# A fourth PV ahead of the second half, and first scores within the projections: a fused attention and SwiGLU layer on one core

## The chip, the cores and the metric

The kernel runs on one core of a Trainium2 chip. The metric is device time in microseconds of one execution, the median of several runs. The engines are named as in the profile: PE (matmuls), PEld (PE's weight loads), DVE (vector), ACT (scalar, activations), POOL (GpSimd) and SP (which issues most DMAs; "SPq" and "ACTq" are the issuing of DMAs).

## The reference

```python
# x [1, 2048, 576], wqkv [576, 1728], wo [576, 576], w1 and w3 [576, 4608], w2 [4608, 576], all bf16
xn = layernorm(x)
q, k, v = heads(xn @ wqkv)                  # 32 heads of 18
s  = q @ k.T * 18 ** -0.5                   # causal, window of 256 keys
A  = concat(softmax(s) @ v) @ wo
B  = (silu(xn @ w1) * (xn @ w3)) @ w2
out = x + A + B
```

## The kernel before

The 2048 tokens are done in four chunks of 512. A chunk has these stages on PE, in this order:

1. The projections (`proj_part`, L437): four pairs of q and k tiles, four of v, and one last k tile, in the order of `PROJ` (L462): q0, q1, v0, q2, v1, q3, v2, 8, v3. Every projection is cut in two parts: the second part of one is issued behind the first part of the next. They use pairs of 64-row tiles of the array.
2. Gate/up (`unit_pairs`, L668): 36 units, each nine pairs of 64-row matmuls of 512 columns. ACT takes a tanh of a unit's gate (`unit_tanh`), DVE makes hT of it with two operations (`unit_h`).
3. The second half (`p2_list`, `p2_item`): full-array matmuls hT by w2 (L719) and oT by wo (L725), 288 columns each, for two halves of the output columns and four blocks of 128 tokens. The wo matmuls come at the end of each half. Four PSUM banks, `ACC`, hold the four sums.

The attention of the chunk is woven into this stream. The heads go in 8 groups of 4. A group has 5 score steps (4 in chunk 0); a step is a few matmuls of 64-row tiles (`scores`, L561) into two fixed banks `SC` = (6, 7), an exp on ACT (`exps`, L570), and masks on POOL (`masks`, L597). Two groups share one PV (`pv`, L618: 96 small matmuls of tiles of 64 rows by 20 columns, 72 in chunk 0). So there are four PVs in a chunk, and behind each a chain on DVE and POOL (`pv_out`, `o_scale`, `o_turn`) and DMAs (`o_pack`) that bring the result into oT, which the wo matmuls read.

A planner written into the kernel sets the order at build time, with a `clock` that counts pairs of 512 columns. It puts a score step into the stream when the clock has passed `nxt`; `nxt` begins at `start`, and the steps are spread so that they are done by `last`:

```python
            start = 20 if c == 0 else 46
            last = total - 12
```

The check stands once behind each entry of `PROJ` (L903 to L917) and ahead of every pair of gate/up. The first three PVs are placed between gate/up units; the fourth stands within the second half, behind its 20th item, in banks taken from a ring of the last two units' banks.

The other six banks form three pairs, `JOBS`, that `job()` hands out in turn to projections, units and PVs.

Before a group can be scored, its queries and keys are moved by DMA: DVE and ACT copy a q pair from PSUM to `stage`, then `repack_span` moves them: `span_main` (L502) and `span_last` (L533). For group 0 these are two DMAs on ACT for the queries, with the semaphore q_0, and four on SP for the keys, with the semaphore k_0; they are issued when q0's second part has been recorded, and the first score of a later chunk waits for all of them. Instructions of one engine run in the order in which they were recorded.

Of the kernel before, what the change touches and what calls it, by code (L numbers as in the profile page):

```python
# [44 lines left out]
class _Prog:  # L45
# [13 lines left out]
    def add(self, eng, fn, r=(), w=(), j=(), dma=None, after=()):  # L59
        deps = []  # L60
        for k in r:
            deps += self.bufs[k].writers
        for k in w:
            g = self.bufs.get(k)
            if g is not None:
                deps += g.ahead(eng)
        for k in j:
            g = self.bufs[k].before
            if g is not None:
                deps += g.ahead(eng)  # L70
        op = _Op(eng, fn, deps + list(after), dma)
        op.after = tuple(after)
        self.n[eng] += 1
        op.pos = self.n[eng]
        if dma is not None:
            self.dma_count[dma] = self.dma_count.get(dma, 0) + 16
            op.cnt = self.dma_count[dma]
        for k in r:
            self.bufs[k].readers.append(op)
        for k in w:  # L80
            self.bufs[k] = _Gen([op], self.bufs.get(k))
        for k in j:
            self.bufs[k].writers.append(op)
        for k in w:
            if self.bufs[k].before is not None:
                self.bufs[k].before.before = None
        self.ops.append(op)
        return op
# [76 lines left out]
def bass_parallel_sum__sliding_block__glu_gated_swiglu__prompt_kernel(  # L165
# [21 lines left out]
    NF = F // 128  # L187
# [10 lines left out]
    with ExitStack() as es:  # L198
# [32 lines left out]
        def pt_slot(sl):  # L231
            kind, n = sl
            if kind == "pt":
                return pt[:, n, :, :]
            if kind == "sh":
                two = stage[:, 2 * n:2 * n + 2, :]
            else:
                two = hT[:, NF - 8 + 2 * n:NF - 6 + 2 * n, :]
            return two.rearrange("p t c -> p (t c)").rearrange("p (q r) -> p q r", r=2)

        def pt_keys(sl):
            kind, n = sl
            if kind == "pt":
                return [("pt", n)]
            if kind == "sh":
                return [("sh", 2 * n), ("sh", 2 * n + 1)]
            return [("h", NF - 8 + 2 * n), ("h", NF - 7 + 2 * n)]
# [16 lines left out]
        PS = es.enter_context(nc.psum_tensor("ps", [128, 8, 512], dt.float32))  # L264
        JOBS, SC = ((0, 1), (2, 3), (4, 5)), (6, 7)
        ACC = [4, 5, 6, 7]
        ring_of = [0, 1, 2, 3]
        ring_ctr = 2
        job_ctr = 2

        def ring():
            nonlocal ring_ctr
            i = ring_of[ring_ctr % 4]
            ring_ctr += 1
            return i

        def job():
            nonlocal job_ctr
            i = job_ctr % 3
            job_ctr += 1  # L280
            return JOBS[i]
# [13 lines left out]
        def load_x(t, eng="sp"):  # L295
            nonlocal xp_ctr
            s = xp_ctr % NXP
            xp_ctr += 1
            add(eng, lambda e: e.dma_start(xp[s][:], x2[t * 128:(t + 1) * 128, :]), w=[("xp", s)], dma=f"xp{s}")
            return s  # L300
# [239 lines left out]
        def keep_keys(g):  # L540
            add("pool", lambda e: e.tensor_copy(
                kb4[:, g, :, :].bitcast(dt.float32), kv[:, g, 2 * NB - NV:NB, :].bitcast(dt.float32)),
                r=[("k", g)], w=[("kp", g)])
# [3 lines left out]
        def steps_of(c):  # L547

            if c == 0:
                return [[(0, 0, 5), (5, 5, 3)], [(1, 1, 5), (6, 6, 2), (7, 7, 1)],  # L550
                        [(2, 2, 5), (4, 4, 2)], [(3, 3, 5), (4, 6, 2)]]
            return [[(0, 0, 5), (-2, 0, 3)], [(1, 1, 5), (5, 5, 3)], [(2, 2, 5), (-3, 0, 2), (-4, 0, 1)],
                    [(3, 3, 5), (6, 6, 2), (7, 7, 1)], [(-1, 0, 4), (4, 4, 4)]]
# [46 lines left out]
        def pv(c, j, banks):  # L600

            seen = set()
            n_all = sum(len(st) for st in steps_of(c))
            n = 0
            for s, st in enumerate(steps_of(c)):
                col = 0
                for kb, q0, nb in st:
                    n += 1
                    pos = (c * NB + kb) % NV
                    for gi in range(2):  # L610
                        g = 2 * j + gi
                        sl = pt_of[(c, g, s)]
                        for pr in range(2):
                            for p in range(2):
                                first = (p, gi, pr) not in seen
                                seen.add((p, gi, pr))
                                q = 2 * gi + pr
                                add("pe", lambda e, p=p, q=q, pr=pr, sl=sl, g=g, pos=pos, q0=q0, nb=nb, col=col, first=first, n=n: e.matmul(  # L618
                                    PS[32 * q:32 * q + VW, banks[p], q0 * KB:(q0 + nb) * KB],
                                    va[64 * p:64 * p + 64, pos, g, pr, :],  # L620
                                    pt_slot(sl)[64 * p:64 * p + 64, col * KB:(col + nb) * KB, pr],
                                    start=first, stop=(n == n_all), tile_position=(64 * p, 32 * q), skip_group_check=True),
                                    r=pt_keys(sl) + [("va", pos)], **{"j" if any(k[0] == p for k in seen - {(p, gi, pr)}) or not first else "w": [("ps", banks[p])]})
                    col += nb

        def pv_out(b, i):
            add("dve", lambda e: e.transpose(uqs[i], PS[:, b, :]), r=[("ps", b)], w=uq_keys[i])
# [63 lines left out]
        def p2_list(c):  # L691

            seq = []
            for half in range(2):
                base = c * 2 * NFC + half * NFC
                for fc in range(NFC):
                    sl = (base + fc) % NW2
                    edge = fc == NFC - 1 or (half == 1 and fc == 0)
                    pairs = [(fl, tt) for fl in range(4) for tt in range(TB)]
                    if edge:  # L700
                        pairs = [(fl, tt) for tt in range(TB) for fl in range(4)]
                    for n, (fl, tt) in enumerate(pairs):
                        seq.append(("w2", half, fc, fl, tt, sl, n == len(pairs) - 1))
                        if fc == NFC - 1 and fl == 3:
                            seq += [("wo", half, fc, kd, tt, sl, False) for kd in range(5)]
                            seq.append(("out", half, fc, 0, tt, sl, False))
            return seq
# [142 lines left out]
        for c in range(NC):  # L850
# [6 lines left out]
            total = 9 * NF + len(att) + 3 * PV_COST  # L857
            if c:
                total += 9 * sum(COST[kind] for kind, _ in PROJ)
            start = 20 if c == 0 else 46  # L860
            last = total - 12
            nxt = soon = start
            clock = 0.0
            done = 0
            pv_ready = {}
# [5 lines left out]
            jobs = {}  # L871
# [47 lines left out]
            for u in range(NF):  # L919
# [18 lines left out]
                if next_pv in pv_ready and clock >= pv_ready[next_pv] and next_pv < 3:  # L938
                    j = next_pv
                    next_pv += 1  # L940
                    banks = job()
# [34 lines left out]
                if u == 29:  # L976
                    xs = [load_x(c * TB + tt) for tt in range(TB)]
            assert done == len(att) and next_pv == 3, (done, next_pv)
            ring_of[:] = [*jobs[NF - 2], *jobs[NF - 1]]
            ring_ctr = 0  # L980
            ACC[:] = [*job(), *SC]
            assert len({*ring_of, *ACC}) == 8
            if c + 1 < NC:
                for g in range(G):
                    keep_keys(g)
            banks = ()
            for n, item in enumerate(p2_list(c)):
                p2_item(c, item, xs)
                if n == 3:
                    for u in sorted(side):  # L990
                        for what in side.pop(u):
                            what()
                elif n == 19:
                    banks = (ring(), ring())
                    pv(c, 3, banks)
                    pv_out(banks[0], 0)
                    pv_out(banks[1], 1)
                    o_scale(0)
                    o_turn(6, 0)
                    o_turn(6, 1)  # L1000
                    o_scale(1)
                    o_turn(7, 0)
                    o_turn(7, 1)
                    o_pack(3, "act")
                elif n == 40 and c + 1 < NC:
                    xn_send((c + 1) * TB + 3)
                elif n == 300 and c + 1 < NC:
                    xn_swap(c + 1, ("sp", "sp"))
                elif n in (100, 120) and c + 2 < NC:
                    t = (c + 2) * TB + (n == 120)  # L1010
                    xslot[t] = load_x(t)
# [31 lines left out]
```

## Time and profile before

| | us |
|---|---|
| median of 3 runs | 564.06 |
| lowest, highest | 564.05, 564.6 |
| the profiled execution | 562.96 |
| its span, first to last instruction | 561.3 |

| engine | busy us | share of the span |
|---|---|---|
| PE | 555.2 | 99% |
| PEld | 330.0 | 59% |
| DVE | 315.9 | 56% |
| ACT | 253.3 | 45% |
| POOL | 163.9 | 29% |

PE's granted clock is full throughout. By line, PE is busy 332.3 us with gate/up (L668), 147.1 with the w2 matmuls (L719), 51.2 with scores (L561), 38.3 with the projections (L437) and 24.8 with wo (L725). Overlapping matmuls count once in a group, and their ends are modelled, so a place on PE is best read by the starts of its matmuls. The stages of chunk 1 in the trace: projections from 144.69 us, the first score at 155.29, gate/up's first pair at 158.30, the second half from 240.96, the fourth PV at 243.51, the end at 282.6.

### The profile page before, as it was taken

Reading aid. Unit: us, or ns where it says so; the run is one execution under the profiler, and the core shown is the slowest. Engines: PE = TensorE matmul, PEld = TensorE weight load, DVE = VectorE, ACT = ScalarE, POOL = GpSimd, SP = SyncE. Lnnn points to the kernel's source line nnn. Section 1 sums busy time; section 2 is a strip of 40 time slices with the busy share of each in tenths; the row PEclk is TensorE's granted clock in tenths of the full one; section 3 lists DMA queues with packets and bytes.
Section 4 is the critical chain, followed back from the end, with each engine's and each line's share of the span. In section 5 each row is a group of like instructions: output and inputs, shape, how many; then the busy total and the mean of one; then the engine's idle time right before and its main releaser. Section 6 shows DMA issues by size and latency. Waiting matters only on the chain.

```text
span 561.3 us, 15707 instructions
## 1 busy us (share of the span) xinstructions
PE 555.2 (99%) x6765; PEld 330.0 (59%) x6765; DVE 315.9 (56%) x586; ACT 253.3 (45%) x349; POOL 163.9 (29%) x384
## 2 busy tenths in 40 slices
PE   7999999999999999999999999999999999999998
PEld 3544544677655455477755545547776454555776
DVE  7666788710366778851046668884114567767211
ACT  3476666100286766600038677650004676666000
POOL 6433344400033445430003444533000333433000
PEclk9999999999999999999999999999999999999999
DMA  9986969965566477596546655969563674460552
GB/s 246 220 171 159 205 171 202 226 177 158 130 142 139 113 162 157 130 214 179 158 106 139 161 123 126 162 162 205 156 172 69 137 172 123 123 162 12 138 148 64
DMA packets 126565, 85.83 MB, mean 153 GB/s; under 512 B 33976, under 2 KB 124272, under 8 KB 126496
## 3 DMA queue, kind: packets, MB, share of 16 engines
q1 hardware_dynamic: 124469, 82.39, 63.0%
q10 hardware_dynamic: 2024, 2.43, 1.8%
q8 instruction: 53, 0.87, 0.7%
q14 instruction: 19, 0.13, 0.1%
HBM read 71.29 MB, written 2.36 MB: 131 GB/s over the span
## 4 chain that ended last, share of the span: by engine, by line
PE 97%; DMA 1%; DVE 1%; ACT 0%; ACTq 0%; POOL 0%; SPq 0%; issue 0%
PE ps L668 49%; PE ps L719 25%; PE ps L437 9%; PE ps L561 6%; PE ps L618 4%; PE ps L725 3%; DMA xp<-in_A_x_dram 1%; DVE xn L370 0%; ACT hT L570 0%; ACTq L502 0%; DVE stats L358 0%; DVE stats L360 0%; ACT xnT L389 0%; ACT th L677 0%; POOL rstd L364 0%
## 5 line engine op out<-in xcount | busy, mean ns | idle before, releaser
L668 PE MATMUL ps<-xnT,w 64*128 64x512 bf16 x1400 | 180.7, 376 | 0.0
L668 PE MATMUL ps<-xnS,w 64*128 64x512 bf16 x1120 | 151.6, 376 | 0.0
L719 PE MATMUL ps<-w,hT 128*128 128x288 bf16 x1152 | 147.1, 286 | 0.0
L683 DVE SCALAR_TENSOR_TENSOR gs<-th,ps 128x512 bf16<-128x512 bf16 x144 | 98.0, 680 | 79.6 <-ACT th L677 78.8
L570 ACT ACTIVATE pt<-ps 128x1024 bf16<-128x1024 f32 (+1 forms) x112 | 113.2, 1011 | 65.1 <-PE ps L561 64.6
L719 PEld LDWEIGHTS ps<-w,hT 128*128 128x128 bf16 x1152 | 112.1, 98 | 30.3 <-issue 1.7
L597 POOL TENSOR_TENSOR pt<-pt,mk 128x128 int32<-128x128 int32 (+1 forms) x199 | 80.8, 427 | 87.0 <-ACT pt L570 87.0
L686 DVE SCALAR_TENSOR_TENSOR hT<-gs,ps 128x512 bf16<-128x512 bf16 x144 | 98.9, 687 | 4.9
L668 PEld LDWEIGHTS ps<-xnT,w 64*128 64x128 bf16 x1400 | 64.9, 94 | 61.0 <-issue 0.3
L677 ACT ACTIVATE th<-ps 128x512 bf16<-128x512 f32 x144 | 85.4, 593 | 23.1 <-PE ps L668 22.8
L668 PEld LDWEIGHTS ps<-xnS,w 64*128 64x128 bf16 x1120 | 53.7, 94 | 57.0
L732 DVE TENSOR_TENSOR ofin<-ps,xp 128x288 bf16<-128x288 f32 x32 | 14.7, 458 | 119.7 <-PE ps L725 119.7
L450 ACT ACTIVATE stage<-ps 128x512 bf16<-128x512 f32 x16 | 9.6, 597 | 145.6 <-PE ps L437 143.2
L597 POOL TENSOR_TENSOR hT<-hT,mk 128x128 int32<-128x128 int32 (+1 forms) x31 | 12.4, 422 | 162.4 <-ACT hT L570 162.4
L561 PE MATMUL ps<-qv,kv 64*128 64x320 bf16 (+4 forms) x528 | 51.2, 260 | 0.1
L561 PEld LDWEIGHTS ps<-qv,kv 64*128 64x128 bf16 x528 | 25.3, 94 | 28.3 <-ACT pt L570 0.6
L437 PE MATMUL ps<-xnT,wp 64*128 64x512 bf16 (+1 forms) x360 | 38.3, 355 | 0.0
L570 ACT ACTIVATE stage<-ps 128x1024 bf16<-128x1024 f32 x24 | 24.6, 1024 | 12.6 <-PE ps L561 12.6
L640 DVE STREAM_TRANSPOSE od<-oq 128x256 bf16<-128x256 bf16 x64 | 25.8, 427 | 6.3 <-POOL oq L633 6.3
L437 PEld LDWEIGHTS ps<-xnT,wp 64*128 64x128 bf16 x360 | 17.4, 94 | 15.6 <-issue 0.7
L725 PE MATMUL ps<-wo,oT 128*128 128x288 bf16 x160 | 24.8, 286 | 0.0
L633 POOL TENSOR_TENSOR oq<-uq,rden 128x288 bf16<-128x288 f32 x16 | 10.8, 676 | 40.1 <-DVE rden L632 40.1
(58 smaller groups left out, 343.6 us busy)
## 6 DMA issues: line engine op xcount, KB each, us to landing
w<-in_B_w_dram SPq DMA_DIRECT2D x210, 192.0 KB, 4.2
w<-in_B_w_dram SPq DMA_DIRECT2D x72, 288.0 KB, 3.2
xp<-in_A_x_dram SPq DMA_DIRECT2D x28, 144.0 KB, 3.8
out_dram<-ofin SPq DMA_DIRECT2D x32, 72.0 KB, 2.1
xnS<-xnT SPq DMA_DIRECT2D x8, 256.0 KB, 4.8
oT<-od SPq DMA_DIRECT2D x48, 36.0 KB
pt<-in_A_wqkv_dram SPq DMA_DIRECT2D x4, 288.0 KB, 8.2
hT<-in_B_w_dram SPq DMA_DIRECT2D x6, 192.0 KB, 3.9
```

The lines of the kernel that those rows point to most:

```text
L437: op = add("pe", lambda e, out_=out_, st=st, mv=mv, n=n, r0=r0, first=first: e.matmul(out_, st, mv, start=first, stop=(part == 1 and n == ...
L561: add("pe", lambda e, r0=r0, out_=out_, kb=kb, q0=q0, nb=nb: e.matmul(out_, kb4[r0:r0 + 64, g, kb + NV - NB, :] if kb < 0 else kv[r0:r0 + ...
L570: add("act", lambda e: e.activation(pt_slot(sl)[:, 0:w, :], PS[:, SC[0]:SC[1] + 1, 0:w].rearrange("p r q -> p q r"), ACT.Exp, scale=scale) ...
L597: add("pool", lambda e, vb=vb, mm=mm: e.tensor_tensor(vb, vb, mm, ALU.mult), r=(key if n == 0 else []) + ["mk"], **{"w" if n == 0 else "j" ...
L618: add("pe", lambda e, p=p, q=q, pr=pr, sl=sl, g=g, pos=pos, q0=q0, nb=nb, col=col, first=first, n=n: e.matmul(PS[32 * q:32 * q + VW, banks ...
L640: add("dve", lambda e: e.transpose(od[i][:, g % 2, c0:c0 + CH // 2], oq[:, c0:c0 + CH // 2]), r=["oq", "oq0"], **{"j" if half or g % 2 els ...
L668: op = add("pe", lambda e, n=n, r0=r0, r=r, k=k, src=src: e.matmul(PS[:, b0 + r, :], wt[r0:r0 + 64, k, fl * 128:(fl + 1) * 128], src, star ...
L677: add("act", lambda e: e.activation(th[i][:], PS[:, bg, :], ACT.Tanh, scale=0.5), r=[("ps", bg)], w=[("th", i)])
L683: add("dve", lambda e: e.scalar_tensor_tensor(out=gs[i][:], in0=th[i][:], scalar=1.0, in1=PS[:, bg, :], op0=ALU.add, op1=ALU.mult), r=[("t ...
L686: add("dve", lambda e: e.scalar_tensor_tensor(out=hT[:, u, :], in0=gs[i][:], scalar=0.5, in1=PS[:, bu, :], op0=ALU.mult, op1=ALU.mult), r= ...
L719: add("pe", lambda e: e.matmul(bank, hT[:, f, tt * 128:(tt + 1) * 128], w2[sl][:, k, :], start=(f == 0), stop=False), r=[("h", f), ("w2", ...
L725: add("pe", lambda e: e.matmul(bank, oT[:, k, tt * 128:(tt + 1) * 128], wo[:, k, d0:d0 + HD], start=False, stop=(k == 4)), r=[("oT", j) fo ...
```

## The change

The fourth PV of a chunk moves from within the second half to directly behind gate/up. It takes the next pair of `job()` for its banks, and the sums of the second half take the banks of the last unit but one and the two score banks. The ring is gone. What follows the PV (`pv_out` to `o_pack`) is issued behind the 4th item of the second half instead of the 20th. In chunks 1 to 3 the planner's `start` is 30 instead of 46, and in all chunks `last` lies 12 units earlier. No matmul is added or taken away.

```diff
         JOBS, SC = ((0, 1), (2, 3), (4, 5)), (6, 7)
         ACC = [4, 5, 6, 7]
-        ring_of = [0, 1, 2, 3]
-        ring_ctr = 2
         job_ctr = 2
-
-        def ring():
-            nonlocal ring_ctr
-            i = ring_of[ring_ctr % 4]
-            ring_ctr += 1
-            return i
...
-            start = 20 if c == 0 else 46
-            last = total - 12
+            start = 20 if c == 0 else 30
+            last = total - 24
...
-            ring_of[:] = [*jobs[NF - 2], *jobs[NF - 1]]
-            ring_ctr = 0
-            ACC[:] = [*job(), *SC]
-            assert len({*ring_of, *ACC}) == 8
+            assert clock >= pv_ready[3], (clock, pv_ready)
+            banks = job()
+            ACC[:] = [*jobs[NF - 2], *SC]
+            assert len({*banks, *jobs[NF - 1], *ACC}) == 8
+            pv(c, 3, banks)
             if c + 1 < NC:
                 for g in range(G):
                     keep_keys(g)
-            banks = ()
             for n, item in enumerate(p2_list(c)):
                 p2_item(c, item, xs)
                 if n == 3:
                     for u in sorted(side):
                         for what in side.pop(u):
                             what()
-                elif n == 19:
-                    banks = (ring(), ring())
-                    pv(c, 3, banks)
                     pv_out(banks[0], 0)
                     pv_out(banks[1], 1)
                     o_scale(0)
```

In the changed kernel all lines of the functions named here have numbers lower by 8.

## The prediction

> **What bounds the kernel now.** I read the page first, then the waits of PE, then timelines around the two places that the change touches: the start of chunk 1's projections at 145 us and the end of its gate/up at 241 us. Chunks 2 and 3 were read the same way.
>
> The page, its first part and the chain that ended last:
>
> ```profile
> PE 555.2 (99%) x6765; PEld 330.0 (59%) x6765; DVE 315.9 (56%) x586; ACT 253.3 (45%) x349; POOL 163.9 (29%) x384
> ...
> PE 97%; DMA 1%; DVE 1%; ACT 0%; ACTq 0%; POOL 0%; SPq 0%; issue 0%
> ```
>
> The matmul engine is the whole kernel: 99% busy, 97% of the chain. No other engine is over 56%. So only two things can move the time: PE streaming less, or PE waiting. The waits of PE's matmuls, all that there are:
>
> ```profile
> PE ps L382 <- DVE xn L370: 1.3, 2, 0.7
> PE ps L754 <- DVE oq L749: 1.2, 1, 1.2
> PE ps L437 <- ACT xnT L389: 0.5, 2, 0.3
> ```
>
> All three lie before 13 us. (The weight loads show waits of 3.0 us ahead of the PVs too, but every one of those PVs starts at the same distance from the matmul before it, so they cost nothing.) After that I measured every matmul's start against the one before it. A pair of 512 columns takes 0.216 us and one of 288 columns 0.1225 us, without exception but for one wait of 0.26 us at 32.1 us (a score behind an exp) and about 0.1 us wherever PE changes the shape of its tiles. The changes of shape around the second half of chunk 1 (PE's timeline, three narrow windows; start us, us):
>
> ```profile
> 240.64 0.38 PE L668 MATMUL ps<-xnT,w 64*128 64x512 bf16 x2
> 240.96 0.42 PE L719 MATMUL ps<-w,hT 128*128 128x288 bf16 x2
> ...
> 243.29 0.29 PE L719 MATMUL ps<-w,hT 128*128 128x288 bf16 x1
> 243.51 0.32 PE L618 MATMUL ps<-stage,va 64*20 64x320 bf16 x4
> ```
>
> Gate/up (64-row tiles) to the second half (full tiles): 0.312 us from start to start where 0.216 is streaming, so +0.096. Second half to PV (64 x 20 tiles): 0.216 against 0.1225, +0.093. PV back to the second half costs about +0.10, and the second full matmul after each entry into L719 comes 0.01 late.
>
> Now the place where the first score of a later chunk will go. Chunk 1 starts its projections at 144.69 us. The keys of group 0 go from PSUM through stage into kv by four DMAs on SP; its queries by two on ACT:
>
> ```profile
> 147.92 0.60 ACT L450 ACTIVATE stage<-ps 128x512 bf16<-128x512 f32 x1 [43.89 <-PE ps L437]
> 147.96 0.69 DVE L449 CAST stage<-ps 128x512 bf16<-128x512 f32 x1 [2.70 <-PE ps L437]
> 148.54 2.59 SPq L502 DMA_DIRECT2D kv<-stage  x3
> 148.55 1.50 ACTq L502 DMA_DIRECT2D qv<-stage  x2
> 151.18 0.77 SPq L533 DMA_DIRECT2D kv<-stage  x1
> ...
> 152.24 0.38 PE L437 MATMUL ps<-xnT,wp 64*128 64x512 bf16 x2
> ...
> 155.29 0.30 PE L561 MATMUL ps<-qv,kv 64*128 64x320 bf16 x2
> ```
>
> SP takes 0.8 to 0.9 us for each issue, so the fourth is issued at 151.18 us. The first score now starts at 155.29 us. The row at 152.24 us is the first matmul of the last q projection, and the instruction order of the changed kernel puts the first score exactly ahead of it. The DMA traffic in the 1.00 us from 152.24 us (40 slices of 25 ns, busy tenths):
>
> ```profile
> DMA  0000000000000044665656210000000000000000
> ```
>
> That burst, 152.57 to 152.85 us, is the fourth DMA's data. The trace's semaphore records have the two q DMAs done at 151.32 us, the first three k DMAs at 150.91, 151.69 and 152.36 us, and the fourth at 153.20 us: 2.02 us after its issue, 0.96 us after the score's new place.
>
> **The change, part by part.**
>
> *Fourth PV moved ahead of the second half.* Before, each chunk has gate/up to sums, sums to PV, PV to sums. After, it has gate/up to PV, PV to sums. Gate/up to PV is known from the other twelve PVs: 0.306 us against 0.216, +0.090. Saved: 0.096 + 0.093 - 0.090 + 0.01 = 0.11 us a chunk, 0.44 us over four. The PV's own 96 matmuls (72 in chunk 0) stay the same, 1.30 and 0.98 us.
>
> Rule beside row: the Trainium skill, "TensorEngine Tiling (Array Packing)", Key Properties, says that a change of tiling mode drains the engine; "TensorE: Matmul & The Clock Gate", Single matmul latency, gives a warm fixed part of about 166 ns, so an undivided drain would be worth, as an estimate from that page, 4 x 0.166 = 0.66 us. The net would be +2.33 us by it. The trace's 0.09 us a change decides.
>
> What could wait there: the PV needs the last group's exps and masks. The last score now stands 5.2 to 7.3 us ahead of the PV, and score to masked tile takes about 2.4 us in the trace (score 163.49, exp 163.91 to 164.93, mask to 165.48). The PV's banks were unit 33's, emptied at 101.75 us in chunk 0, with the PV at 103.3. The sums' first banks are now those of unit 34, whose last VectorE reader ends at 104.00 us in chunk 0. The sums come at 103.32 + 0.98 = 104.30 us there, 0.5 us or more after that reader in the other chunks. So no wait, by a margin of 0.25 us.
>
> *PV's tail.* Transposes, reciprocals and the six oT DMAs on ACT are issued one to three us earlier, in a stretch where ACT has nothing else. They are needed only at the first wo matmul (120.5 us in chunk 0; issues now end at 116.2). Nothing is gained, PE never waited for them. SP's order at this place is unchanged, but the first w2 refill waits for slot 0, read out 1.3 us later. In chunk 2 it was issued at 381.10 us, landed at 387.49, and is due at 388.1. Its new issue is about 382.2, but it landed behind a backlog (w13 parts until 385.67), so I take no wait; with the full shift it would cost about 0.5 us, once.
>
> *Score steps, last = total - 24.* No score is added. A score step streams in 0.213 us between 64-row matmuls of the same shape, without a change of tiles, wherever it stands. Spacing stays about 1.95 us, the same as now, where exp (1.02 us) and tanh (0.59 us) fit. Cost: 0.
>
> *First score, start 46 to 30.* The planner's clock passes 30 after v1 has begun, at 34.9, where it passed 46 after v2 had begun, at 48.9. That is 3.05 us earlier. PE executes in order, so the score's wait for k_0 (all four DMAs) holds everything: q3, v2, 8, v3 and gate/up queue behind it. What feeds the four DMAs (q0's evacuation, SP's queue, idle from 146.3 to 148.54) is upstream of the wait, so an earlier score does not bring them forward. The trace of before has no PE wait on a DMA in a later chunk, so the price is bounded. Below: only three DMAs in time, 152.36, would give 0.17 us a chunk. Above: the same line's DMA in chunk 0, issued at 23.96 and done at 27.14, took 3.18 us, which gives 2.17 us a chunk. I take the chunks' own rows, as they are the same DMAs in the same place: done at 153.20, 291.15, 429.06 us; score due at 152.24, 290.20, 428.13 us; and 0.05 us from semaphore to matmul (the release at 32.05 us had its matmul at 32.09). 1.01 + 1.00 + 0.98 = 2.99 us. Chunk 0 keeps its start of 20. Nothing later gives it back: PE has no other wait that a delay could swallow.
>
> Sum: 2.99 - 0.44 = +2.55 us. The profiled execution took 562.96 us (span 561.3 and 1.66 around it), giving 565.5. The median of the runs shown is 564.06, 1.1 above the profiled one, so 566.6 us, +0.45%.
>
> **The rivals.**
>
> Keys in time: the DMAs would have to be done 0.96 us earlier. For it: three of four nearly are. Against: four issues in a row on one queue, the same within 0.03 us in three chunks. Then only the switches count: 564.06 - 0.44 = 563.6, no measurable change. The wait outweighs the switches from 0.15 us a chunk. 5%.
>
> Keys later still: SP or the transfers slower, as in chunk 0; 3 x 1.16 us more, 570.1. 7%.
>
> A second wait: the exp (1.02 us) now stands in ACT between the evacuations of q2 and v1, the w2 refill or unit 34's bank is late. Each is 0.3 to 0.5 us, in one to three chunks: 567 to 568. Against: the scores at 155.29 and 157.59 us have the same neighbours and cost nothing. 15%.
>
> The clock: if each wait let PE's clock fall to the start-up rate (512 columns 0.427 us apart until 5.06 us, for 3.4 us), each would lose 1.7 us more: 571.7. Against it, the gap of 1.36 us before 6.42 us was followed by matmuls at full rate (288 columns, 0.12 us). 2%. The Trainium skill, "TensorE: Matmul & The Clock Gate", What's actually happening, asks for an idle window of about 3.4 us; that gap agrees.
>
> Faster by over 1.1 us: it needs no wait and all three changes of shape gone (0.29 us a chunk, 1.2 us). Two of them stay in the order. 2%.
>
> **How the numbers follow.** The forecast has 69%. Range 565.4 to 568.1: below, waits of 0.6 us a chunk; above, a second wait of 0.5 us in each of three chunks. It leaves out the keys in time, most of the late keys, the clock and the faster case, some 15%. A change under 0.2% (1.1 us) is about what a measurement of this kernel cannot tell from none. Slower: 69 + 7 + 15 + 2 = 93%; same 5%; faster 2%.
>
> **What would show it.** In the changed profile: PE's waits gain a group L553 behind a kv DMA, three times about 1 us, with PE idle at the third q projection's end in chunks 1 to 3; 0.31 us from gate/up to PV, no L711 to L610 change; no wait at the second half's start. I am wrong if the first score runs without a gap after q2, or if PE waits at the PV.

## The result, and the profile after

The changed kernel takes 568.33 us (median of 21 runs, 566.12 to 574.28), the kernel before 563.51 us in runs beside it (21, 562.3 to 567.42). The ratio is 1.0083, with a 95% interval of 1.0066 to 1.0101: slower by 4.8 us. (A ratio here is taken over all runs, so it can differ a little from that of the medians.) The direction is as forecast, but the loss is nearly twice the forecast 2.55 us, and 568.33 lies 0.2 us above the range. The changed kernel's executions also spread over 8 us. One profile is therefore one draw: the profiled execution took 566.73 us (span 565.0), 3.8 us over the profiled one of before. That it lies near the forecast 566.6 is luck, as its sum below shows.

The page of after, its engines and the chain that ended last, by engine and by line:

```profile
PE 555.7 (98%) x6765; PEld 329.9 (58%) x6765; DVE 314.3 (56%) x586; ACT 255.0 (45%) x349; POOL 163.4 (29%) x384
...
PE 95%; DMA 3%; ACT 1%; DVE 1%; SPq 1%; issue 0%; ACTq 0%; POOL 0%
PE ps L660 48%; PE ps L711 25%; PE ps L429 8%; PE ps L553 6%; PE ps L610 3%; PE ps L717 3%; DMA kv<-stage 2%; DMA xp<-in_A_x_dram 1%; ACT xnT L381 0%; SPq L494 0%; SPq L525 0%; ACT hT L562 0%; PE ps L374 0%; ACTq L494 0%; DVE stage L441 0%
```

PE's busy time grew by 0.5 us, while the span grew by 3.7: what was added is mostly waiting. The DMAs from stage into kv, which the chain of before did not have, now hold 2% of it. The waits of PE's matmuls:

```profile
PE ps L553 <- DMA kv<-stage: 4.0, 4, 1.5
PE ps L746 <- DVE oq L741: 1.2, 1, 1.2
PE ps L374 <- DVE xn L362: 0.7, 1, 0.7
PE ps L429 <- ACT xnT L381: 0.2, 1, 0.2
```

The first line is the wait that was forecast, with two differences: four times, not three, and a longest of 1.5 us. Chunk 1's, in the timeline:

```profile
151.22 0.78 SPq L494 DMA_DIRECT2D kv<-stage  x1
...
152.05 0.76 SPq L525 DMA_DIRECT2D kv<-stage  x1
...
152.25 1.03 PE L429 MATMUL ps<-xnT,wp 64*128 64x512 bf16 x8
...
154.11 0.31 PE L553 MATMUL ps<-qv,kv 64*128 64x320 bf16 x2 [0.84 <-DMA kv<-stage]
```

The fourth key DMA is issued at 152.05 us and the score starts 2.06 us later. Four pairs of 512 columns start from 152.25 us, so the score would have followed at 153.11: from start to start it waits 1.00 us. The bracket's 0.84 is shorter because the profile lets the matmul before it end later. All waits below are from start to start. The score waits 1.00, 1.00 and 0.98 us in chunks 1 to 3 (forecast 1.01, 1.00, 0.98). The fourth wait is chunk 0's, whose first score the change leaves where it was:

```profile
26.03 0.81 PE L660 MATMUL ps<-xnT,w 64*128 64x512 bf16 x6
28.36 0.39 PE L553 MATMUL ps<-qv,kv 64*128 64x320 bf16 x4 [1.52 <-DMA kv<-stage]
```

This is 1.69 us, where before had none. In the other profiles it is absent, or anything up to 1.99 us.

The order around the fourth PV is as forecast (PE's timeline, two narrow windows in chunk 1):

```profile
242.45 0.38 PE L660 MATMUL ps<-xnT,w 64*128 64x512 bf16 x2
242.76 0.32 PE L610 MATMUL ps<-stage,va 64*20 64x320 bf16 x4
...
243.59 0.59 PE L610 MATMUL ps<-pt,va 64*20 64x128 bf16 x32
244.12 0.30 PE L711 MATMUL ps<-w,hT 128*128 128x288 bf16 x1
```

Gate/up to PV is 0.31 us, PV to sums runs on, and nothing waits there. The sum for this execution: key waits 2.98, changes of shape -0.44, chunk 0's score 1.69, two short waits of w2 matmuls together 0.21, and start-up projections that begin 0.8 earlier: +3.6, against the 3.7 measured. Of this only 2.5 is the forecast. The median, 4.8 us over before, asks for more, and so does the spread. The experiments turned to the w2 matmuls.

### The profile page after: what moved, and what is told of

It reads as the page before. It is cut to its first block, busy times and chain, and to the rows that moved or that the text cites. A ratio compares the mean times of both kernels' runs of the same rounds, so it can differ in the third digit from the quotient of the medians.

```text
span 565.0 us, 15707 instructions
## 1 busy us (share of the span) xinstructions
PE 555.7 (98%) x6765; PEld 329.9 (58%) x6765; DVE 314.3 (56%) x586; ACT 255.0 (45%) x349; POOL 163.4 (29%) x384
## 4 chain that ended last, share of the span: by engine, by line
PE 95%; DMA 3%; ACT 1%; DVE 1%; SPq 1%; issue 0%; ACTq 0%; POOL 0%
PE ps L660 48%; PE ps L711 25%; PE ps L429 8%; PE ps L553 6%; PE ps L610 3%; PE ps L717 3%; DMA kv<-stage 2%; DMA xp<-in_A_x_dram 1%; ACT xnT L381 0%; SPq L494 0%; SPq L525 0%; ACT hT L562 0%; PE ps L374 0%; ACTq L494 0%; DVE stage L441 0%
## 5 line engine op out<-in xcount | busy, mean ns | idle before, releaser
L711 PE MATMUL ps<-w,hT 128*128 128x288 bf16 x1152 | 146.6, 286 | 0.0
L711 PEld LDWEIGHTS ps<-w,hT 128*128 128x128 bf16 x1152 | 112.1, 98 | 29.3 <-DMA w<-in_B_w_dram 0.5
```

What stands on the lines that cost most here:

```text
L711: add("pe", lambda e: e.matmul(bank, hT[:, f, tt * 128:(tt + 1) * 128], w2[sl][:, k, :], start=(f == 0), stop=False), r=[("h", f), ("w2", ...
```

## Experiments

The kernels of one series ran on one chip beside the kernel before. Every ratio is against the before of its own series; the medians of these lie between 563.41 and 563.73 us. "PV ahead" is the changed kernel's placing of the fourth PV and its banks. E is the time when the last gate/up pair of a chunk has streamed (its start and 0.216 us). Counts of the planner are in its own unit, pairs of 512 columns: `last` lies 12 such pairs earlier in the changed kernel, 2.6 us of streaming, not 12 gate/up units.

**1. The parts.** `early_only` is the kernel before with the first scores early; `pv_only` is the changed kernel without that; `after_again` is the changed kernel itself; `after_w2five` gives it a fifth w2 slot, taken from the buffers of exps; chunk 0 may use four other buffers in return.

```diff
# early_only, from before
-  start = 20 if c == 0 else 46
+  start = 20 if c == 0 else 30
# pv_only, from after
-  start = 20 if c == 0 else 30
+  start = 20 if c == 0 else 46
# after_w2five, from after
-  NXP, NOF, NPT, NW13, NW2, NOD = 7, 4, 10, 3, 4, 2
+  NXP, NOF, NPT, NW13, NW2, NOD = 7, 4, 9, 3, 5, 2
...
-  if c:
-      free += [("sh", n) for n in range(4)]
+  free += [("sh", n) for n in range(4)]
...
-  if c == 0 and u in (20, 22, 24, 26):
+  if c == 0 and u in (18, 20, 22, 24, 26):
```

> The kernel before with start = 30 alone: early first scores, the fourth PV still behind the 20th item of the second half. Theory (w2): three key waits of 1.0 us, +3.0 us, as tight as before, and w2 refills landing about 1 us ahead of their use as before. Rival (keys): +5 us in the median with the changed kernel's wide spread.

> The changed kernel with start = 46 again in chunks 1 to 3: the fourth PV ahead of the second half and last = total - 24, without the early first score. The profiled runs show the changed kernel's three key waits as forecast (1.00, 1.00, 0.98 us), so 2.98 us must go with them. Theory (w2): the rest of the loss, about 2 us of the median and the wide spread (566.1 to 574.3 us), is PE waiting for the first w2 refill at the fifth block of the second half in chunks 0 to 2, since the PV now stands ahead of the block that frees the slot; then this kernel keeps it: 0.4 us gained by the changes of tile shape, 2 us lost in the median, so about +1 to +2 us against before, with a spread of several us and w2 waits in the profile. Rival (keys): the rest is key waits that are longer in other executions; then this kernel is at -0.4 us, as tight as before. Rival (chunk 0): the rest is the first score of chunk 0 waiting for its keys (1.7 us in the profiled run), which the change does not touch; then -0.4 us as well.

> The changed kernel unchanged, for a second profile on the chip of the others. All theories: +4 to +5.5 us in the median, executions spread over some 5 us. Theory (w2): the fifth block of the second half waits in some of chunks 0 to 2, by another amount than in the first profile (0.08, 0.00, 0.13 us there). Rival (keys): the waits ahead of the first scores differ from 1.0 us.

> The changed kernel with five w2 slots in place of four (one more load ahead in chunk 0; room made by 9 pt slots for 10, with the four stage slots used in chunk 0 too). The first refill is then due at the sixth block, 1.96 us later. Theory (w2): the w2 waits go, the key waits of 3 x 1.0 us stay: +2.6 us, tight. Rival (keys): no change against the changed kernel, +4.8 us and the same spread.

Measured: `early_only` 566.34 us, ratio 1.0056 (1.0035 to 1.0076), with three key waits of 0.98 to 1.00 us in its profile, and one of 0.10 us for w2 in chunk 1. `pv_only` 566.33, ratio 1.0048 (1.0027 to 1.0068), 563.41 to 569.98. `after_again` 567.73, ratio 1.0085 (1.0052 to 1.0118). `after_w2five` 566.7, ratio 1.0072 (1.0043 to 1.01).

So the key waits cost the 2.9 us that they were priced at, and the part that was to save 0.44 us costs about as much again. The two together, 2.9 and 2.9, are more than what the whole costs (4.3 in this series, 4.8 at first), by no more than these spread medians leave open. Where the second part's cost lies, the profile of `after_again` shows. The longest group of PE's waits, and two rows of the timeline of chunk 0's second half:

```profile
PE ps L711 <- DMA w<-in_B_w_dram: 2.6, 3, 1.6
```

```profile
114.36 2.13 PE L711 MATMUL ps<-w,hT 128*128 128x288 bf16 x16 [1.62 <-DMA w<-in_B_w_dram]
116.72 0.54 PE L711 MATMUL ps<-w,hT 128*128 128x288 bf16 x3 [0.23 <-DMA w<-in_B_w_dram]
```

PE waits for w2. The kernel holds four blocks of w2 and refills a slot when its 16 matmuls are read. The fifth block, the first refill, was issued at 106.89 us and landed at 114.31. In the changed kernel's first profile it was issued at 107.34, landed at 113.06, and was used 0.05 us later. In before it was 106.74, 111.09, and a margin of 1.17. From start to start `after_again` waits 1.79, 0.40 and 0.11 us in chunk 0 and 0.91 in chunk 1: 3.2 us. `after_w2five`'s profiled execution (565.87) has the key waits and no w2 wait, and four of its six runs, this one among them, lie between 565.87 and 566.73; the other two, 568.76 and 571.63, are not explained. Its median is 3.2 us over before where 2.6 and a tight spread were expected.

**2. What holds the refill back.** Two edits take transfers out of its way. `pv_defer` and `after_defer` issue the six w13 parts that follow the 32nd gate/up unit, loaded for the next chunk, within the second half instead of ahead of it. `pv_xnt_late` issues the next chunk's first xn transposes later. `pv_w2five` is the fifth slot on `pv_only`.

```diff
# pv_defer, from pv_only; after_defer, the same from after
-  if u % 4 == 3 and u < NF - 4 and (c or u != 15):
+  if u % 4 == 3 and u < NF - 8 and (c or u != 15):
...
+  elif n in (160, 182, 204, 226, 248, 270):
+      load_part()
# pv_xnt_late, from pv_only
-  elif n == 40 and c + 1 < NC:
+  elif n == 110 and c + 1 < NC:
```

> pv_only (fourth PV ahead, start = 46) with the six w13 parts that are issued behind unit 31 moved into the second half (items 160 to 270). In the profiles so far the first w2 refill lands in the order of issue behind a queue of w13 and x transfers that have taken 5 to 8 us each to land. Theory (w2 behind a backlog): without these 1.2 MB ahead of it the refill takes 3 to 4.5 us, no wait is left in the second half, and the kernel gains the 0.11 us a chunk: -0.4 us (-0.07%), as tight as before. Rival (something else in the moved PV: its chain of POOL and DVE, the oT transfers): the spread and the +2 to +3 us of pv_only stay. Rival (moved load): w13 or w2 waits elsewhere, +0.5 us or more.

> The changed kernel with the same deferral of w13. Theory: the three key waits alone are left: +2.55 us (+0.45%), tight, the figure of the prediction. Rival (something else in the moved PV): as the changed kernel, +4.3 to +4.8 us.

> pv_only with five w2 slots. Theory: due 1.96 us later, the refill lands in time in most executions: -0.4 us, with a few late ones as in the changed kernel with five slots (568.8 and 571.6 us there). Rival (something else in the moved PV): median +2 to +3 us as pv_only.

> pv_only with the last DMA transpose of xn (issued behind item 40) moved behind item 110. If that transpose is what holds the refills: -0.4 us. If the w13 and x transfers ahead of the refill hold it (the theory), this changes nothing: +2 to +3 us as pv_only, since the transpose is issued behind the first two refills.

Measured: `pv_defer` 563.16 us, ratio 0.9999 (0.9986 to 1.0012). `after_defer` 566.95, ratio 1.0056 (1.004 to 1.0072). `pv_w2five` 564.16, ratio 1.0006 (0.9992 to 1.002). `pv_xnt_late` 564.74, ratio 1.0019 (1.0002 to 1.0036): 1.0 us over before, between its two expectations, so it tells little. All of PE's waits in `pv_defer`:

```profile
PE ps L746 <- DVE oq L741: 1.2, 1, 1.2
PE ps L374 <- DVE xn L362: 1.0, 2, 0.7
PE ps L429 <- ACT xnT L381: 0.4, 2, 0.2
```

The group L711 is gone: chunk 0's first refill is issued at 106.11 us, lands at 109.30 and has a margin of 2.5. With six transfers of 192 KB out of the queue, this refill takes 3.2 us, where it took 3.9 to 6.1 in the profiles of `pv_only` and 5.7 and 7.4 in those of the changed kernel. The extra cost of the PV part goes with it. `after_defer` keeps 3.2 us of loss, whose interval (2.2 to 4.1) holds the 2.55 that the key waits would leave; its profile has no w2 wait of 0.2 us or more. So the w2 waits come from the queue ahead of the refill.

**3. Which part of the change fills that queue.** My theory then was the refill's lost lead: with the PV ahead, slot 0 is read out with no PV behind it, so the refill has 1.3 us less until its use. `refill_late` takes that lead from the kernel before. `last_only` takes the other part of `pv_only`, the score steps done 12 pairs earlier. `before_defer` is the deferral on before, and `best` is `pv_defer` with chunk 0's first score ten pairs later, against that score's wait.

```diff
# refill_late, from before: chunk's first refill waits for the fourth PV
-  if last:
+  if last and (half or fc):
...
+  load_w2((last_pe(),))      # behind pv(c, 3, banks)
# last_only, from before
-  last = total - 12
+  last = total - 24
# best, from pv_defer
-  start = 20 if c == 0 else 46
+  start = 30 if c == 0 else 46
```

> The kernel before, with the first w2 refill of each second half made to wait for the end of the fourth PV (it waited for the first block of 16 sums), so that it is issued about 5.4 us ahead of its use. In the profiles the time from issue to use in chunks 1 to 3 was 6.7 to 7.1 us before and 5.3 to 5.8 us with the PV ahead. Theory (lost lead): that lead alone, with the PV in its old place, costs +1.5 to +3 us in the median and brings the spread of several us. Rival (something else in the moved PV): no change, within 0.5 us of before.

> The kernel before with last = total - 24 alone (scores and the first three PVs earlier, the fourth PV in its old place). Theory: no change, within 0.5 us, and tight; the first refills keep 6.7 to 7.1 us from issue to use in chunks 1 to 3. Rival (the denser scores and the earlier PVs shift the transfers): +1 us or more with a spread.

> The kernel before with the six w13 parts behind unit 31 moved into the second half. Theory: no wait to remove there in most executions, so 0 to -0.5 us; the kernel with the PV ahead and the same deferral lies 0.44 us below this one. Rival (the deferral itself is the gain of that kernel): this one is as fast as it or faster.

> The version that the runs point to: fourth PV ahead, start = 46 in later chunks, w13 deferred, and start = 30 in chunk 0 too, whose first score waited for its keys in some profiles (1.69 and 1.99 us with start = 20, 0.50 and 0 in others). Expected 562.5 to 563.2 us, 0.5 to 1.0 us below before. If the first score of chunk 0 rarely waits, it is only 0.4 us below.

Measured: `refill_late` 563.3 us, ratio 0.9994 (0.9978 to 1.0011). `last_only` 564.35, ratio 1.0021 (0.9995 to 1.0046), with runs up to 569.05, where before reaches 567.19 beside it. `before_defer` 563.46, ratio 0.9998 (0.9981 to 1.0014). `best` 562.67, ratio 0.9981 (0.9965 to 0.9997), all 12 runs within 562.14 to 563.41, and no wait of a score in its profile.

The lost-lead theory falls: with the lead gone, issue to use was 5.2 us, the transfers took 3.3 to 4.8, and nothing waited. `last_only`, with neither the new PV nor a new wait by design, has a slow tail, but its interval holds no change, and its profiled execution (563.03 us, its lowest) has one w2 wait of 0.09 us. Deferral does nothing for before, so it mends something that before does not have.

**4. The two halves of the second part, apart.** `pv_last12` is the PV ahead with the score steps left where they were; `last_refill_late` has the early score steps and the lost lead in the old place of the PV. `pv_only` and `last_only` are run again beside them.

```diff
# pv_last12, from pv_only
-  last = total - 24
+  last = total - 12
-  assert clock >= pv_ready[3], (clock, pv_ready)
# last_refill_late: refill_late's edit and last_only's
```

> pv_only again, on the chip of the next three. All theories: +1.5 to +3 us in the median, spread of several us.

> The kernel before with last = total - 24. Theory (queue): the earlier third PV takes a pause out of SP's issues ahead of the x and w13 transfers, so the queue that the refill joins drains later; some executions lose 1 to 5 us, median +0.5 to +1 us. Rival (lead): nothing, as the refill keeps its lead.

> last = total - 24 and the first refill made to wait for the end of the fourth PV, which stands in its old place. Theory (both together): +2 to +3 us as pv_only_2. Theory (queue alone): as last_only_2, +0.5 to +1 us, since the refill lands behind the w13 parts in the order of issue whenever it is issued.

> The fourth PV ahead of the second half with last = total - 12 and start = 46: scores where they were before. The last masks end 0 to 2 us ahead of the PV, so it may wait for them in chunk 3 by up to 0.5 us. Theory (queue): with SP's order as before, no w2 waits of size: -0.4 to +0.3 us, tight. Rival (the PV ahead by itself): +2 to +3 us with the spread.

Measured: `pv_last12` 562.82 us, ratio 0.9994 (0.9982 to 1.0006). `last_only_2` 565.01, ratio 1.0027 (1.0008 to 1.0047). `last_refill_late` 564.97, ratio 1.0026 (1.0006 to 1.0045). `pv_only_2` 565.5, ratio 1.004 (1.0025 to 1.0055), its profile with w2 waits of 1.69, 0.39 and 0.11 us in chunk 0.

The PV ahead costs nothing by itself; its 0.6 us gain is of the size forecast (0.44), though the interval holds no change. The moved score steps cost 1.6 us by themselves (0.8 in the series of `last_only`), and taking the lead as well adds nothing. Of the kernels with the early steps and the PV in its old place, only `last_refill_late` was profiled above its median (567.59 us): chunk 0's refill lands 11.7 us after E and PE waits 2.68 us for it. What they do that a count of PE's work does not show is on SP. SP's timeline of before, then of after, ahead of chunk 0's second half:

```profile
89.90 2.57 SPq L323 DMA_DIRECT2D w<-in_B_w_dram  x4
94.29 3.08 SPq L655 DMA_DIRECT2D oT<-od  x4
97.42 1.89 SPq L299 DMA_DIRECT2D xp<-in_A_x_dram  x4
```

```profile
91.05 1.26 SPq L315 DMA_DIRECT2D w<-in_B_w_dram  x2
93.02 3.09 SPq L647 DMA_DIRECT2D oT<-od  x4
96.15 1.68 SPq L315 DMA_DIRECT2D w<-in_B_w_dram  x2
97.88 2.02 SPq L291 DMA_DIRECT2D xp<-in_A_x_dram  x4
```

The score steps end earlier, so the third PV of chunk 0 comes one gate/up unit earlier, and with it the four oT DMAs of its `o_pack`. They now stand ahead of two w13 parts instead of behind them. An oT DMA waits for DVE and takes SP 0.77 us, so SP issues no w13 part from 92.31 to 96.15 us; the two parts go out some four us later, counted against E, next to the four x loads and ahead of the refill. `pv_last12`'s SP runs through this stretch in before's order, and it has no w2 wait:

```profile
89.59 2.57 SPq L315 DMA_DIRECT2D w<-in_B_w_dram  x4
93.98 3.08 SPq L647 DMA_DIRECT2D oT<-od  x4
97.11 1.89 SPq L291 DMA_DIRECT2D xp<-in_A_x_dram  x4
```

**5. That order alone.** `pv_opack_late` is `pv_only` with only these four DMAs issued a unit later.

```diff
-  later(u + 3, lambda j=j: (o_turn(2 * j + 1, 1), o_pack(j, "sp")))
+  later(u + 3, lambda j=j: o_turn(2 * j + 1, 1))
+  later(u + 3 + (c == 0 and j == 2), lambda j=j: o_pack(j, "sp"))
```

> pv_only with the four oT DMAs of chunk 0's third PV issued one unit later, so that SP's order up to chunk 3 is that of before. Theory (order on SP): the refill of chunk 0 lands 7.4 to 8.4 us after gate/up's end, in time for its use at 8.8: -0.4 us, tight (562.3 to 564.5). Rival (the scores themselves: exps, masks and PVs at other times): as pv_only, +2 to +3 us with refills at 10.5 us or more in some profiles.

> pv_only on the same chip: +2 to +3 us in the median, spread of several us.

Measured: `pv_only_3` 565.8 us, ratio 1.0046 (1.0027 to 1.0064). `pv_opack_late` 564.24, ratio 1.0012 (1.0 to 1.0024). Its SP's timeline has before's order again:

```profile
91.33 2.80 SPq L315 DMA_DIRECT2D w<-in_B_w_dram  x4
94.17 3.24 SPq L647 DMA_DIRECT2D oT<-od  x4
97.46 1.89 SPq L291 DMA_DIRECT2D xp<-in_A_x_dram  x4
```

Four DMAs moved back by one unit take away 1.6 us of 2.4, and the two intervals do not meet, so by the medians their place is most of the cost. The profile of `pv_opack_late` does not show how, and its expectation was missed there: in this execution (565.15, above its median) chunk 0's refill lands 9.9 us after E, not 7.4 to 8.4, and PE waits 1.01 us for it, and 0.71 in chunk 1:

```profile
PE ps L711 <- DMA w<-in_B_w_dram: 1.4, 2, 0.8
PE ps L553 <- DMA kv<-stage: 1.3, 1, 1.3
```

The second row is chunk 0's first score. So the order is not all. The traces show an effect of the early score steps (`last = total - 24`) that lies ahead of these four DMAs: the w2 load that SP issues some 22 us ahead of chunk 0's E takes 3.7 to 4.1 us to land in the five profiles without the early steps, and 4.9 to 6.0 in the fifteen with them, `pv_opack_late` (6.0) among these. And in chunks 1 and 2 SP's order is that of before in `pv_only` and `last_only` too, yet w2 waits of 0.09 to 0.55 us stand there. No run isolates these two.

## Why the prediction was wrong in size

**Key waits: right** in place, number and size (2.98 us against 2.99). `early_only` alone costs 2.9. Keys in time and keys later still are out. The price of keys later still was misread: 23.96 us is the end of that DMA's issue, which began at 23.18, so it took 3.96 us by the measure that gave 2.02, and the rival's time would be 572.4 us, not 570.1. (Likewise the rows from score 163.49 to mask 165.48 are 2.0 us, not 2.4.) Neither entered the sum.

**Changes of shape: right.** Gate/up to PV is 0.31 us, the L711 to L610 change is gone, and `pv_last12`'s median is 0.6 us under before, which does not contradict 0.44.

**The step that failed** is "Score steps, last = total - 24. ... Cost: 0." It priced the score steps on PE, ACT and the spacing, and did not follow what hangs on them: a PV comes when its steps are done, and its chain, four SP DMAs among it, comes behind the PV. "SP's order at this place is unchanged" was true, but only of the place looked at, the fourth PV. The order differs 10 us earlier, at the third. In place of 0, the early steps cost 0.8 and 1.6 us alone (medians of `last_only`, `last_only_2`; the interval of the first holds no change), and with the PV ahead the cost is 2.1 to 2.9 (`pv_only`, three times) where the PV alone has none. The order on SP is most of that, by `pv_opack_late`; the rest is open.

**The w2 refill, mis-sized.** "I take no wait; with the full shift it would cost about 0.5 us, once." The danger was seen, but from one landing in one profiled execution. The waits come to 0.1 to 3.2 us in the profiles of the changed order that have any, those above 1 us all in chunk 0, though chunk 2 was the one examined. After E the first refill of chunk 0 is due at 9.0 us. Without the early score steps it lands at 7.9 (before), 8.5 (`early_only`), 7.7 (`refill_late`) and 7.5 (`pv_last12`). With them it lands at 9.0, 10.7 (the changed kernel twice), 7.1, 10.6, 7.8 (`pv_only`), 8.1, 7.4 (`last_only`), 11.7 (`last_refill_late`), 9.0 (`pv_xnt_late`) and 9.9 (`pv_opack_late`). The early steps spread the landing; the lost lead decides little. A second wait was a rival with 15%, in this place, "0.3 to 0.5 us, in one to three chunks"; it was part of what happened, and its price was too low: a single refill waited up to 2.7 us. The range's upper end followed from that price.

**The clock, 2%.** A clock that falls in each wait is out: no key wait of 1 us was followed by slow matmuls. But it is not absent, as the last section tells.

Open: how chunk 0's first refill comes to land 7.1 us after E in one execution and 10.6 in another of the same kernel; the remaining 0.8 us of `pv_opack_late` (interval 0 to 1.4); why the early steps cost more with the PV ahead; and why chunk 0's first score waits in some executions. That last wait, 0.3 us or more, stands in six of the twelve profiles with the PV ahead and `start = 20` in chunk 0, and in none of the seven with the PV in its old place. Whether it belongs to the change or to these few draws was not tested; it may be part of the costs above.

The version that gains is `best`: PV ahead, six w13 parts deferred, chunk 0's first score later. Its ratio of 0.9981 is about the smallest difference that can be told here, and its spread of 1.3 us is the smallest of all.

## What to carry to other kernels

When an edit moves a step, compare the order of every issuing queue over the whole stretch that the planner rearranges, not only at the step: a DMA that waits for a compute engine holds the loads behind it, and the load that pays can be due some 20 us later. A buffer whose refill lands within about a microsecond of its use in one profile has no cover; read the margin in all stages, and write the range for its loss. If a change widens the spread of the executions, the fastest profile does not show why: profile again until a slow one is caught.

## What the runs showed of the hardware

One wait slowed the clock. In `last_refill_late`'s profile the w2 wait of chunk 0 is 2.68 us from start to start. PE's timeline, and the stretches around it (busy time and count of PE, PEld, DVE, ACT and POOL, granted clock, DMA share, GB/s; the share is summed over packets and can pass 1):

```profile
111.83 0.78 PE L719 MATMUL ps<-w,hT 128*128 128x288 bf16 x5
115.12 5.15 PE L719 MATMUL ps<-w,hT 128*128 128x288 bf16 x27 [2.51 <-DMA w<-in_B_w_dram]
```

```profile
112.00:116.00 4.00, 1.49 (x13) 0.96 (x12) 0.00 (x0) 0.00 (x0) 0.00 (x0) 1.00 1.62 237
116.00:119.40 3.40, 3.40 (x17) 2.15 (x15) 0.00 (x0) 0.00 (x0) 0.00 (x0) 0.50 0.77 168
119.40:123.00 3.60, 3.60 (x31) 2.88 (x30) 0.00 (x0) 0.00 (x0) 0.00 (x0) 1.00 0.71 191
```

From 116.00 us, 0.88 us after PE had resumed, the granted clock is 0.50 for 3.4 us: 17 matmuls where the next 3.6 us hold 31. Fifteen matmuls came 0.240 us apart instead of 0.1225, which adds 1.8 us to the wait. Waits of 1.0 to 2.0 us had no such row. The Trainium skill, "TensorE: Matmul & The Clock Gate", What's actually happening, puts the idle window that drops the clock to half at about 3.4 us, in windows that run freely. The half rate and the length of the slow stretch agree; but here a wait of 2.68 us was enough. In 3 of the changed kernel's 21 runs the mean granted clock was 0.997, and one such stretch, 3.4 us at half rate in a span of 566, is a mean of 0.997; so these runs probably hold one, though no profile caught it there. `pv_only` has four such runs of 12 in each of two series; `pv_last12`, `pv_defer` and `best` have none, and before has three of 35 in the series of `best`.

Loads issued on SP landed in the order of their issue wherever these traces tell their landing, and a 288 KB refill took 3.2 us behind an emptier queue (`pv_defer`) and 7.4 us behind a full one (`after_again`).
